# A listed order for the first two token groups, and no unused products at the end

## The chip, the cores and the metric

The kernel runs on one core of a Trainium2 chip. The metric is the device time of one execution in microseconds (us). A core has five engines that work side by side, each through its own instructions in the order in which they were issued: TensorE (PE) for matrix products and transposes, VectorE (DVE), ScalarE (ACT) and GpSimd (POOL) for element-wise work, and SyncE (SP), which here issues the DMA transfers. An engine that comes to an instruction whose input is not ready waits, and everything behind it on that engine waits too. The order of each engine is therefore a design decision of the kernel, and it is what this change is about.

## The reference

The inputs are q, k and v of shape (4, 8, 768, 64), one decay factor per head, and two weight matrices, w_in (512 x 2048) and w_out (2048 x 512). First comes a linear attention with decay, in blocks of 64 tokens:

```python
for b in range(nb):                                   # 12 blocks of 64 tokens
    intra = einsum('bhic,bhjc->bhij', qb, kb) * Dmask # decayed scores inside the block
    intra = einsum('bhij,bhjd->bhid', intra, vb)
    inter = einsum('bhid,bhde->bhie', qb * lam_pow, kv_state)
    out[:, :, sl] = intra + inter
    kv_state = lam_block * kv_state + einsum('bhsd,bhse->bhde', kb * rev_pow, vb)
```

The result is reordered into x, 3072 tokens x 512, and goes through a two-layer network:

```python
h = x @ w_in                  # 3072 x 2048
g = np.maximum(0.01 * h, h)   # leaky relu
return g @ w_out              # 3072 x 512
```

The weights come as float64. The kernel reads them as 64-bit words and builds float32 values from the two halves. Products run in a fast float32 form (fp32r) on operands that are split into a main part (h), a rest (l) and a difference (m), so that one product of the reference becomes three on TensorE.

## The kernel before

**Tiling.** The tokens are cut into 24 chunks of 128 and six groups of four chunks (512 tokens). The 2048 columns of the hidden layer are cut into eight panels of 256.

**Attention.** For a chunk, SP loads k, q (L338, two DMAs each) and v (L388, one DMA). PE transposes k and q (L403; k into a bank b11 or po, q into pt). ACT copies the transposed tiles out (L414 for k, L415 for q), k is multiplied by its decay in place (L419), and q by its powers (L423). PE then makes the scores and the state products into one bank pair, psc (L313, in function scores). DVE multiplies the scores with the decay matrix (L452, into the tile sc), copies or adds the state (L457, L459), and POOL decays the state for the next block (L462). PE makes the outputs into the bank pair po (L313, in function outputs): the block's own part from sc, then in two portions the part from the state, with a tiny copy of po (L491) between the portions. ACT writes the main part of x (xh, L507), DVE the rest and the difference (xl L508, xm L510). From chunk 10 on, k and q are loaded as small sub-blocks instead (L374, many DMAs of 32 or 48 KB) and transposed by DVE (L383).

**Weights of w_in.** For a panel there are two loads of 512 KB (L566). ACT writes three words or half words of each (L578, L580, L582), DVE shifts and adds (L584, L585). The main part of the panel is written by ACT or DVE (wh, L591 or L593), rest and difference by DVE (wl L596, wm L602).

**The first layer, "up".** An up step for a group and a panel (L640) makes two banks out of b10, b11 and b2. Per bank there are products of the h parts and of the l parts, then a scaling by ACT (L658), then products of the m parts, then the leaky relu by ACT (L661) into one of two buffers gs. SP stores the buffer to DRAM (L664, tile g, 512 KB). The two gs buffers alternate, so a leaky relu must wait until the store two steps back has left its buffer.

**The second layer, "down".** From about 340 us on, g is loaded (L675), split (ACT L682, DVE L683 and L685) and multiplied (L700). The results go through ACT L722 and DVE L729 and are stored (L732), at the very end in two stores of half a tile. Before that, w_out is converted like w_in, written to DRAM (L617) and read back (L621) when it replaces the panels of w_in.

**What sets the order.** No engine instruction is issued when its line of Python runs. `add` puts it in a plan with its engine (or a choice of engines), an assumed duration, and the names it reads and writes, and the plan gives it a rank. `emit` then places operations one after the other: each time the one that could start first by the assumed durations, at equal times the one of lower rank. The PE operations of one attention round form a chain, which is kept together: once its first operation is placed, PE takes nothing else until the last. After that, every operation is issued in the order of its assumed start.

**Unused work on PE.** Where the plan sees PE without work before the first product into b10, it puts in unused transposes of 128 x 128 (L266, into b10). There are 30 of them, beside those ahead of the plan. After the last result, 24 unused products of 512 columns (L802) and 8 small ones (L809; 16 rows in the profile) run.

```python
if self.idle is not None and t > soon[e] + 0.4:
    self.idle(int((t - soon[e] - 0.2) / 0.22))
```

## Time and profile before

| what | value |
|---|---|
| median of three runs | 611.83 us (611.01 to 612.28) |
| span of the profiled execution | 610.3 us |
| its own time | not measured apart; the median exceeds its span by 1.5 us |
| mean granted clock of TensorE | 0.997 |
| PE busy | 601.9 us (99%) |
| DVE, ACT, POOL busy | 313.2 us (51%), 269.9 us (44%), 86.6 us (14%) |
| PE idle | 8.4 us, of which 6.6 before 35 us |
| first product of the up steps | starts at 30.41 us |
| scores times decay (L452) of chunks 0 to 3 | start at 8.80, 14.10, 19.04, 26.05 us |
| last result product of PE | ends at 606.28 us |
| last unused product | ends at 609.39 us |

The span runs from the first to the last instruction that the profiler recorded; an execution's time holds a little more. A busy share is the share of the span in which an engine executes something; a matrix product counts as busy until its modelled end. "Granted clock" is the share of full speed at which TensorE was allowed to run. A row such as `L313 <- DMA att<-in_v_dram` names the waiting line and what it waited for. In an instruction's name the tile written stands left of the arrow; att is one large tile that holds all of the attention's data, so a row with att must be told by its line.

### The profile page before, as it was taken

What the parts mean: (1) busy time and instruction counts of PE and PEld (TensorE: products, weight loads), DVE (VectorE), ACT (ScalarE), POOL (GpSimd) and SP (SyncE); (2) the same over time, 40 slices, a digit from 0 to 9 for tenths busy, and PEclk for the clock granted to TensorE, in tenths of its full rate; (3) what the DMA queues carried; (4) which work ended last, traced back from release to release, by engine and by line L of the source; (5) the groups of instructions that cost most, each with busy time, mean ns of one, the idle gap of its engine ahead of it and who ended that gap; (6) DMA issues with size and microseconds to landing.
All of it is one profiled execution on the core that took longest, in us unless ns stands there. A gap on an engine that the chain in (4) does not pass through costs nothing.

```text
span 610.3 us, 13012 instructions
## 1 busy us (share of the span) xinstructions
PE 601.9 (99%) x5426; PEld 497.6 (82%) x5426; DVE 313.2 (51%) x418; ACT 269.9 (44%) x430; POOL 86.6 (14%) x90
## 2 busy tenths in 40 slices
PE   7799999999999999999999999999999999999999
PEld 5688888888888878888788888888888888888887
DVE  5899764334243426326366755545454544636531
ACT  4678974444455646555577522222222313214111
POOL 2564412114133004104000000000000000000000
PEclk9899999999999999999999999999999999999999
DMA  9999775666889878886686843524333343333201
GB/s 201 236 261 263 215 204 126 175 154 176 192 212 245 212 222 219 212 242 212 233 302 219 278 155 103 173 69 139 137 104 134 111 136 111 132 104 126 82 1 69
DMA packets 147754, 105.18 MB, mean 172 GB/s; under 512 B 123632, under 2 KB 124400, under 8 KB 147696
## 3 DMA queue, kind: packets, MB, share of 16 engines
q1 hardware_dynamic: 147552, 104.36, 58.8%
q8 instruction: 42, 0.69, 0.5%
q14 instruction: 16, 0.13, 0.1%
q10 hardware_dynamic: 144, 0.00, 0.0%
HBM read 68.69 MB, written 35.65 MB: 171 GB/s over the span
## 4 chain that ended last, share of the span: by engine, by line
PE 95%; DMA 2%; ACT 1%; DVE 1%; issue 0%; SPq 0%; ACTq 0%
PE b L640 42%; PE b L700 18%; PE po L700 11%; PE psc L700 11%; PE po L313 4%; PE psc L313 4%; PE pt L700 4%; DMA g<-gs 1%; DMA att<-in_v_dram 1%; PE pt L403 1%; DMA att<-in_q_dram 1%; PE po L403 0%; PE psc L802 0%; ACT att L415 0%; PE b L266 0%
## 5 line engine op out<-in xcount | busy, mean ns | idle before, releaser
L682 ACT ACTIVATE xh<-att 128x1024 fp32r<-128x1024 f32 x48 | 50.8, 1060 | 149.1 <-PE b L700 133.6
L683 DVE SCALAR_TENSOR_TENSOR xl<-att,xh 128x1024 fp32r<-128x1024 f32 x48 | 58.7, 1223 | 97.5 <-ACT xh L682 97.5
L640 PE MATMUL b<-xm,wm 128*128 128x512 f32 (+2 forms) x392 | 104.5, 392 | 0.7 <-ACT b L658 0.7
L640 PE MATMUL b<-xh,wh 128*128 128x512 f32 (+2 forms) x392 | 103.2, 386 | 0.8 <-ACT xh L507 0.8
L640 PE MATMUL b<-xl,wl 128*128 128x512 f32 (+2 forms) x392 | 103.4, 387 | 0.0
L640 PEld LDWEIGHTS b<-xh,wh 128*128 128x128 f32 x392 | 72.9, 188 | 16.0 <-ACT xh L507 0.9
L640 PEld LDWEIGHTS b<-xl,wl 128*128 128x128 f32 x392 | 72.7, 188 | 15.1 <-DVE wl L596 0.3
L640 PEld LDWEIGHTS b<-xm,wm 128*128 128x128 f32 x392 | 71.4, 188 | 16.0 <-ACT b L658 1.1
L658 ACT ACTIVATE b<-b 128x512 f32<-128x512 f32 (+2 forms) x97 | 56.1, 580 | 60.6 <-PE b L640 60.5
L661 ACT ACTIVATE gs<-b 128x512 f32<-128x512 f32 (+2 forms) x97 | 57.0, 592 | 44.2 <-PE b L640 38.3
L700 PE MATMUL b<-wh,xh 128*128 128x512 f32 x192 | 74.7, 389 | 0.0
L700 PE MATMUL b<-wl,xl 128*128 128x512 f32 x192 | 74.7, 389 | 0.0
L685 DVE SCALAR_TENSOR_TENSOR xm<-xl,xh 128x1024 fp32r<-128x1024 f32 x48 | 58.7, 1225 | 4.7
L462 POOL TENSOR_TENSOR att<-att 128x256 f32<-128x256 f32 x40 | 34.4, 861 | 58.7 <-DVE att L459 58.7
L700 PEld LDWEIGHTS b<-wh,xh 128*128 128x128 f32 x192 | 36.1, 188 | 7.5
L700 PEld LDWEIGHTS b<-wl,xl 128*128 128x128 f32 x192 | 36.0, 188 | 7.5
L423 POOL TENSOR_TENSOR att<-att 128x512 f32<-128x512 f32 (+1 forms) x20 | 25.3, 1265 | 95.6 <-PE po L313 34.7
L452 DVE TENSOR_TENSOR att<-psc,att 128x512 f32<-128x512 f32 x24 | 16.5, 689 | 43.1 <-PE psc L313 43.1
L584 DVE TENSOR_SCALAR w<-w 128x512 int32<-128x512 int32 x32 | 19.6, 612 | 36.0 <-ACT w L578 35.9
L700 PE MATMUL psc<-wh,xh 128*128 128x512 f32 x96 | 37.3, 389 | 0.0
L700 PE MATMUL psc<-wl,xl 128*128 128x512 f32 x96 | 37.3, 389 | 0.0
L700 PE MATMUL psc<-wm,xm 128*128 128x512 f32 x96 | 37.3, 389 | 0.0
(79 smaller groups left out, 810.4 us busy)
## 6 DMA issues: line engine op xcount, KB each, us to landing
att<-g SPq DMA_DIRECT2D x48, 512.0 KB, 3.3
g<-gs SPq DMA_DIRECT2D x47, 512.0 KB, 4.0
raw<-in_moe_w_in_dram SPq DMA_DIRECT2D x16, 512.0 KB, 5.5
raw<-in_moe_w_out_dram SPq DMA_DIRECT2D x16, 512.0 KB, 4.8
att<-in_k_dram SPq DMA_DIRECT2D x48, 128.0 KB, 4.3
att<-in_v_dram SPq DMA_DIRECT2D x24, 256.0 KB, 4.5
out_dram<-gs SPq DMA_DIRECT2D x23, 256.0 KB, 2.1
wo<-w SPq DMA_DIRECT2D x8, 512.0 KB, 5.9
```

Of the source, the lines that this page charges most:

```text
L313: nc.tensor.matmul(dst[HALF[cols]], lhsT=lhsT[HALF[rows]], rhs=rhs[HALF[rows]], start=start, stop=True, skip_group_check=True)
L423: add(eng, us, lambda: e.tensor_tensor(o, x, _bc(pow_q, 2, 2)[:, :, m, :], op=ALU.mult), ["fq", dep], [f"qsT{i}"])
L452: add("DVE", 0.69, lambda: nc.vector.tensor_tensor(sc, psc[:, :, lower, :], decay, op=ALU.mult), ["psc", "fk"], ["sc"])
L462: add("POOL", 0.7, lambda new=new, j=j: nc.gpsimd.tensor_tensor(state[(j + 1) % 4], new, _bc(lam_c, 2, D), op=ALU.mult), [f"st{j % 4}", "f ...
L584: add("DVE", 0.42, lambda: nc.vector.tensor_scalar(d, d, 3, None, op0=ALU.logical_shift_left), [], [key])
L640: nc.tensor.matmul(dst, lhsT=w[z][:, kk * 2 * P + f * P:kk * 2 * P + (f + 1) * P], rhs=x[z][:, kk, toks], start=start and kk == 0, stop=kk ...
L658: add("ACT", ns, lambda b=b: nc.scalar.activation(out=b, in_=b, func=AF.Copy, bias=0.0, scale=S + 1.0), [], [kb], rank=-1.5)
L661: add("ACT", ns, lambda b=b, r=r: nc.scalar.activation(out=r, in_=b, func=AF.Prelu, bias=0.0, scale=1.0 / WS, alpha=0.01), [kb], [f"gs{jg} ...
L682: add("ACT", 1.05, lambda: nc.scalar.activation(out=h, in_=graw[j], func=AF.Copy, bias=0.0, scale=NEAR), reads, wr("h"))
L683: add("DVE", 1.25, lambda: nc.vector.scalar_tensor_tensor(l, graw[j], 1.0, h.bitcast(F32), op0=ALU.mult, op1=ALU.subtract), reads + [f"rh{ ...
L685: add("DVE", 1.25, lambda: nc.vector.scalar_tensor_tensor(m, l.bitcast(F32), -S, h.bitcast(F32), op0=ALU.mult, op1=ALU.add), [f"rh{j}", f" ...
L700: nc.tensor.matmul(acc[tb][z // 2][:, cols], lhsT=ring[j][z][:, f * T + tb * P:f * T + (tb + 1) * P], rhs=W[pp][z][:, f * d_model:(f + 1) ...
```

## The change

1. A list ORDER names the first 707 operations of the plan (by number, with the engine where there is a choice): all loads, attention rounds, conversions and up steps up to the end of the up steps of groups 0 and 1, with what the list has beside them. `emit` places these first, in this order, each as soon as its inputs and its engine allow by the assumed durations, and then goes on as before with what is left. The issue order of every engine in about the first 200 us is thus the listed one, and what follows is placed from another state of the plan.
2. The attention rounds that the list touches are no longer kept together on PE: transposes and products of other steps can stand between their parts.
3. Unused transposes come only where the list says so (an entry fN puts N of them before the next PE operation): 31 instead of 30.
4. The second set of decay factors is ordered behind the first.
5. The unused products at the end (L802 and L809) are removed.
6. A table OWN is prepared that could give chunks their own buffers; it is empty, and so changes nothing.

Read off the changed program, the loads that SP issues first are q, k, k, q of chunks 0 and 1 and then v of chunk 0, where they were k, q, v, k, q. The numbers and kinds of the other instructions stay. The lines move down by 53 to 58, so L313 becomes L366, L452 L505, L640 L698 and L658 L716.

```diff
+ORDER = """
+3 2 25 0 26 f3 6 4 1 8 f2 5 100 7 9p 10 27 f3 11 49 28 30 f2 12 29 14 48 102 13 15 101 94 16 f1 18 31 104 17 19
+103 32v 50 34 20a 21 33 35 22 23 105 52 37 71 36 51 38 95 72 39 41 56 53 40 42 54 73 43v 98 55 f1 44 96 24 57
...
+637 682 636 699 663 703 503 668 704 571 700 661 640 695 705 641 659 664 678 676 656 706 683 653 671 662 660 672
+673 679
+"""
...
+        self.listed, self.fill = [], {}
...
+        first = {i for i, _ in self.listed}
         for c in self.chains.values():
+            if first.intersection(c):
+                continue
             m = [i for i in c if "PE" in self.ops[i][0]]
...
+        for i, e in self.listed:
+            e = e or next(iter(self.ops[i][0]))
+            assert i in able[e]
+            put(i, e, max(free[e], since(i, e)))
+        while len(done) < n:
...
-                if self.spare in self.ops[i][4]:
+                if self.spare in self.ops[i][4] and not self.listed:
                     self.idle = None
-                if self.idle is not None and t > soon[e] + 0.4:
+                if i in self.fill:
+                    self.idle(self.fill[i])
+                elif not self.listed and self.idle is not None and t > soon[e] + 0.4:
                     self.idle(int((t - soon[e] - 0.2) / 0.22))
...
-    add("DVE", 1.25, factors_q, [], ["fq"])
+    add("DVE", 1.25, factors_q, ["fk"], ["fq"])
...
+    fill = 0
+    for x in ORDER.split():
+        if x[0] == "f":
+            fill = int(x[1:])
+            continue
+        i = int(x.rstrip("avp"))
+        plan.listed.append((i, {"a": "ACT", "v": "DVE", "p": "POOL"}.get(x[-1])))
+        if fill and "PE" in plan.ops[i][0]:
+            plan.fill[i], fill = fill, 0
     plan.emit()
-    a, b = ring[0][0], W[0][0]
-    spare = acc[0] + acc[1]
...
-    strips(2, 6)
-    strips(4, 3)
-    f = graw[0]
-    for _ in range(4):
-        for i in range(2):
-            nc.tensor.matmul(spare[2][HALF[i], 0:C2], lhsT=f[:, 0:C2], rhs=f[:, 0:C2], start=True, stop=True, skip_group_check=True)
```

85 lines of the change are left out of this document (57 added, 28 removed).

## The prediction

> **What bounds the kernel now.** I read the page's busy times first, then the 40 slices, then the waits of TensorE, the table of stretches, and last the timelines of the stretches that were not full.
>
> ```profile
> PE 601.9 (99%) x5426; PEld 497.6 (82%) x5426; DVE 313.2 (51%) x418; ACT 269.9 (44%) x430; POOL 86.6 (14%) x90
> PE   7799999999999999999999999999999999999999
> PEclk9899999999999999999999999999999999999999
> ```
>
> TensorE (PE) is busy for 601.9 of 610.3 us. Only 8.4 us are idle, and the first two slices (to 30.5 us) and the last show it; the lowered clock is early too. The stretches say this in numbers (columns: stretch, length, busy us of PE, PEld, DVE, ACT, POOL, granted clock, DMA share, GB/s):
>
> ```profile
> 15.00:20.00 5.00, 4.33 (x140) 3.25 (x139) 4.61 (x8) 3.78 (x8) 2.64 (x3) 1.00 1.02 227
> 20.00:25.00 5.00, 3.19 (x109) 2.47 (x112) 3.91 (x7) 3.18 (x6) 4.20 (x4) 1.00 1.02 262
> 25.00:30.00 5.00, 4.62 (x115) 3.80 (x104) 3.95 (x6) 2.30 (x5) 1.09 (x3) 0.66 0.89 226
> 35.00:50.00 15.00, 15.00 (x232) 12.33 (x231) 14.07 (x19) 12.37 (x23) 6.86 (x5) 1.00 0.88 250
> 600.00:611.00 11.00, 9.39 (x72) 7.28 (x70) 2.14 (x4) 1.79 (x3) 0.00 (x0) 1.00 0.26 95
> ```
>
> From 35 to 600 us PE idles 0.96 us in all (0.68 in 200-250, 0.28 in 250-300). From 0 to 35 the busy times add up to 28.4, so 6.6 us are idle there. So an order can gain ahead of the first up product (30.41 us) and at the end; elsewhere it can hardly do anything but lose. What holds PE early (columns: waiter, releaser, total us, times, longest), and the way to the first product:
>
> ```profile
> PE psc L313 <- DMA att<-in_v_dram: 1.8, 1, 1.8
> PE psc L313 <- DVE att L459: 1.6, 2, 1.1
> PE b L640 <- ACT xh L507: 0.8, 1, 0.8
> ```
>
> ```profile
> 24.43 1.57 PE L313 MATMUL psc<-att 64*64 64x64 f32 x64 [1.79 <-DMA att<-in_v_dram]
> 25.93 1.33 PE L266 MATMUL b<-att 128*128 128x128 f32 x5
> 27.19 1.46 PE L313 MATMUL po<-att 64*64 64x64 f32 x48
> 28.58 0.66 PE L403 MATMUL pt<-att 128*128 128x128 f32 x4
> 29.16 0.46 PE L313 MATMUL po<-att 64*64 64x64 f32 x16
> 30.41 1.43 PE L640 MATMUL b<-xh,wh 128*128 128x512 f32 x5 [0.78 <-ACT xh L507]
> ```
>
> Chunk 3's state products wait 1.79 us for a v that is the 23rd load on SP's queue; behind them come unused transposes, chunk 3's outputs, a later chunk's transposes and the copy xh. The same shapes are slower here than elsewhere (psc x64 1.57 against 1.09 at 35.26, po x48 1.46 against 0.93 at 20.39, an unused transpose 0.27 in the five here against 0.16 in three at 7.63): the granted clock was halved from 25.0 to 28.4.
>
> **The change, part by part.** The sum is made against the profiled execution: its span is 610.3, and with the 1.5 us by which the median of the runs (611.83) exceeds it, its time is 611.8; the lowest and highest run put that 1.5 at 0.7 and 2.0. The instruction mix stays; the real PE work is equal, so the difference is PE idle, lowered clock and tail. Line numbers are those of before.
>
> *First stage.* The way to the first product is one scores-times-decay (L452) per chunk on DVE, ended at 9.49, 14.79, 19.73 and 26.74 before. In the listed order:
> - v of chunk 0 is the 9th load instead of the 5th. With issues about 0.5 apart from 0.74 and a median of 4.5 to landing it is there at 0.74 + 8 x 0.5 + 4.5 = 9.3. State products (about 0.6), a state copy of 0.41 that now stands ahead, then L452 0.69: ends at 11.1, 1.6 later.
> - Chunk 1: between the two L452 DVE now has L459 0.41, L584 0.84 to 1.28 (as beside POOL), L419 0.67, L423 0.69, L508 0.69, L585 0.69, L459 0.41, L452 0.69, less 8 x 0.085 overlap (0.69 at 14.10, the next at 14.71): 4.4 to 4.9. With some 0.3 of waits, 16.3 (1.5 later).
> - Chunk 2: two L459, L423, the seen copy, L584, L510, L585, L508, L452: 4.2 to 4.6 by the same rows, and the second L459 waits for POOL's decay (L462, 0.86): 22.0 (2.3 later).
> - Chunk 3: L596 1.22 to 1.64, L459, L423, L510, L508, L452, less overlaps: 4.4. It ends at 26.4, 0.3 earlier than before: v of chunk 3 is now the 18th load, so the 1.79 wait goes, and DVE is late next.
> - First product: outputs 0.75 for 24 pieces, seen copy 0.16, the rest 0.31, xh 0.59, and five hand-overs of 0.05 to 0.1: about 28.8 against 30.41. L415 (0.59) and four transposes (0.66) have moved behind the copy. That is 1.6 earlier, but four transposes (0.44 at full clock) are still owed: 1.2 gained with a clean clock.
>
> The clock: in this walk PE idles about 14.7-16.4 and 17.3-19.0, where before had 4.33 busy of 5. Before's halving followed 20-25 with 3.19 of 5 busy and cost 1.0 or a little more (0.48 on psc, 0.53 on po, some on the transposes). That is in the 30.41 already; another such stretch takes the gain to -0.1, and one that hits the serial part more turns it to +1.2. I take -0.3, nearer the row of a half-busy PE; ends -1.2 and +1.2. The 31 unused transposes stand for 30 and are the cover that is cut where the list says so.
>
> [...]
>
> *Conversions near 88 us.* The last m product of group 0 with panel 7 needs wm7 (L602). DVE has L584 (released by ACT at about 83.1), L452, L584, two L585, L593 and L602 ahead: 0.42 + 0.69 + 0.42 + 0.69 + 0.69 + 0.69 + 1.22 = 4.8 if alone, and POOL's decays stand beside them. In before no up product waits for DVE at all. PE waits 0.5; ends 0 and 1.2 (L584 at 1.28, L593 at 1.43). [...]
>
> *Stores between 110 and 137 us.* G stores now stand on SP between the small loads of L374 (about 0.5 per issue). Two buffers gs: L661 of an up step waits for the store two steps back, then L658, then PE. Before has this chain at 213.8:
>
> ```profile
> 214.79 5.73 DMA g<-gs
> 220.52 0.02 issue
> 220.54 0.04 ACTq L661
> ...
> 223.35 0.44 ACT gs L661
> 223.79 0.49 ACT b L658
> 224.28 0.04 issue
> 224.33 2.12 PE b L640 x8
> ```
>
> The 5.73 us store cost PE 0.7 there. In the listed stretch the chain closes at a landing of about 3.0 and costs about 2 at the median of 4.0, 3 at 4.5. Stores without small loads beside them took 2.7 to 3.0 in the trace, those with them 3.98 and 4.18. I take 3.4, near the 3.3 median of the 512 KB loads of G, and so 0.8; ends 0 and 3.
>
> *After the list, about 333 us.* The rest is placed greedily, from another state. ACT then gets, between the scalings of two up banks, L591, L578, L580, L582, L682 and L661: 1.06 + 0.66 + 0.78 + 0.77 + 1.06 + 0.60 - 5 x 0.10 = 4.43. Before has only L591, L658, L682, L661 there (331.56 to 334.56, nothing waits), with L578 to L582 one bank earlier. PE has four groups of products to cover it, 4 x 0.907 = 3.63; with two hand-overs it waits about 1.0 (0.8 to 1.1).
>
> *End.* Before, the two last stores land at 608.55 and 609.01, the unused products end at 609.39 and the exit follows. Without them the stores end the kernel: -0.4 (-0.5 to 0). No product follows them, so a lower clock there hurts nothing. The transposes and copies moved within the listed part beyond these places cost nothing, covered by a PE that is full in every stretch of 35 to 200; a cover too thin shows as PE idle there.
>
> Sum: -0.3 + 0.5 + 0.8 + 1.0 - 0.4 = +1.6, so 611.8 + 1.6 = 613.4.
>
> **Rivals.**
> - *Faster: the first stage gains more.* For it: 6.6 of the 8.4 us idle lie there, the v wait is gone, and my walk adds DVE's worst rows at L584. Against it: three L452 come later. It decides when first up products start before about 28.0 at full clock (30.41 - 0.44 - 28.0 = 2.0 gained) and stores land in 3.0: -2.0 + 1.0 - 0.4 = -1.4, 610.4.
> - *No difference: the parts cancel.* Clean clock (-1.2), wm7 in time, stores at 3.2 (0.4), +1.0, -0.4: -0.2, 611.6. This is also the case of an order that moves work PE never waits for.
> - *Clearly slower: the store chain.* Stores at 4.5 give 3 us instead of 0.8; with the rest as summed 615.6. For it: 3.98 and 4.18 beside small loads. Against it: only one 0.7 us wait of this kind in all of before.
> - *The clock.* A second halved stretch of 3.4 us before 30 us costs about 1.1 more: 614.5.
>
> **How the numbers follow.** Likeliest 613.4 (0.40); store chain 0.09 and second halving 0.05 beside it; parts cancel 0.24; faster 0.22. A change within 0.2% (1.2 us, 610.6 to 613.0) can't be told from none. Slower by more 0.54, within 0.24, faster 0.22. The range: low end at the faster rival's first stage taken 0.5 further (products from 27.5), 609.9; high end at +1.2 + 1.2 + 1.5 + 1.1 - 0.4 = +4.6, 616.4. The likeliest case's own range is 613.0 to 614.8.
>
> **What would show it.** First stage: L452 ends near 11, 16, 22, 26.4, the first up product near 28.8, no wait for in_v at chunk 3, and the clock of the slices to 30 us. Conversions: a wait of an up product for DVE's wm L602 near 88. Stores: up products waiting for ACT's L658 between 110 and 140, behind a G store of 4 us or more. Greedy rest: a wait of about 1 us for L658 near 333. End: the last work a store about 1.5 us before the span's end. I am wrong if PE stays full from 35 us on while the first product starts before 28 (faster), or if the first stage alone loses over 2 us.

## The result and the profile after

The changed kernel takes 613.3 us (median of six runs, 612.87 to 614.21), against 611.12 us for the kernel before in the same session (six runs, 610.33 to 612.28). The ratio is 1.0034 with a 95% interval of 1.0024 to 1.0045: slower by about 2.2 us. The time is 0.1 us beside the predicted 613.4, but the forecast stood on a base of 611.8, and six runs put that base at 611.12: the forecast change was +1.6, the measured one +2.2. The profiled execution is one of the six: 613.25 us, span 611.43. From here on lines are those of the changed kernel unless "before" is said: L266 is now L319, L313 L366, L403 L456, L414 L467, L415 L468, L419 L472, L423 L476, L452 L505, L462 L515, L491 L544, L578 L631, L640 L698, L658 L716, L661 L719. (A correction to what stands ahead: the 30 and 31 unused transposes include the 11 that run ahead of the plan.)

The busy times and slices of the page, after:

```profile
PE 600.1 (98%) x5387; PEld 496.0 (81%) x5387; DVE 304.8 (50%) x418; ACT 268.0 (44%) x430; POOL 83.7 (14%) x90
...
PE   7899999999999999999999999999999999999997
...
PEclk9899999999999999999999999999999999999999
```

PE has 1.8 us less work than before, since the unused products are gone; their last slice now shows 7. The second slice is fuller than before (8 for 7), and the lowered clock is still there. The table of stretches, after (columns as before: stretch, length, busy us of PE, PEld, DVE, ACT, POOL, granted clock, DMA share, GB/s):

```profile
15.00:20.00 5.00, 2.60 (x85) 1.88 (x88) 3.41 (x9) 2.95 (x6) 2.25 (x3) 0.99 0.85 171
20.00:25.00 5.00, 4.83 (x133) 4.17 (x127) 4.82 (x9) 2.78 (x5) 2.78 (x3) 0.67 1.06 298
25.00:30.00 5.00, 4.62 (x154) 3.52 (x145) 3.69 (x7) 2.75 (x6) 1.60 (x2) 1.00 1.01 256
35.00:50.00 15.00, 15.00 (x235) 12.34 (x234) 10.57 (x14) 12.52 (x23) 10.71 (x8) 1.00 0.74 190
300.00:350.00 50.00, 49.22 (x217) 40.41 (x217) 30.24 (x31) 32.88 (x53) 0.00 (x0) 1.00 0.75 264
600.00:611.00 11.00, 7.81 (x39) 6.43 (x37) 2.83 (x5) 2.04 (x4) 0.00 (x0) 0.97 0.26 95
```

The half-busy stretch has moved from 20-25 to 15-20, and the halved clock follows it one stretch earlier (0.67 in 20-25, where before had 0.66 in 25-30). From 35 us on PE again hardly idles: the largest hole is 0.78 in 300-350. The waits of PE, after (waiter, releaser, total us, times, longest):

```profile
PE po L366 <- DVE att L544: 1.6, 1, 1.6
...
PE po L366 <- DVE att L505: 1.4, 3, 0.7
PE b L698 <- ACT gs L719: 0.8, 1, 0.8
PE psc L366 <- DMA att<-in_v_dram: 0.6, 1, 0.6
PE psc L366 <- ACT att L468: 0.5, 1, 0.5
```

The 1.79 us wait for chunk 3's v is gone; a wait of 1.58 for DVE, in chunk 1's outputs, stands in its place. The timeline of PE around it and at the first up product, after:

```profile
17.55 0.33 PE L319 MATMUL b<-att 128*128 128x128 f32 x1
19.46 0.46 PE L366 MATMUL po<-att 64*64 64x64 f32 x16 [1.58 <-DVE att L544]
19.74 1.84 PE L366 MATMUL psc<-att 64*64 64x64 f32 x64
...
29.07 0.66 PE L456 MATMUL pt<-att 128*128 128x128 f32 x4
29.85 2.11 PE L698 MATMUL b<-xh,wh 128*128 128x512 f32 x8
```

What DVE waited for is on ACT. ACT's timeline, after:

```profile
16.98 0.68 ACT L631 ACTIVATE w<-raw 128x512 f32<-128x512 f32 x1 [2.60 <-DMA raw<-in_moe_w_in_dram]
17.57 0.56 ACT L467 COPY att<-b 128x512 f32<-128x512 f32 x1
18.03 0.58 ACT L468 COPY att<-pt 128x512 f32<-128x512 f32 x1
```

The list puts a conversion of w_in ahead of the copies of a chunk's k and q. Its load is late, ACT stands 2.60 us, and the copies behind it wait though their own data are ready. DVE's timeline, after:

```profile
18.65 0.69 DVE L476 TENSOR_TENSOR att<-pt,att 128x512 f32<-128x512 f32 x1 [1.46 <-ACT att L468]
19.26 0.15 DVE L544 COPY att<-po 128x2 f32<-128x2 f32 x1
```

On DVE L476 (chunk 2's q) is released by L468 at 18.65, the tiny copy L544 (of chunk 1's outputs) stands behind L476 and ends at 19.41, and PE waits for that.

**Where the 1.14 us of the two profiles lie.** The first product starts 0.56 earlier (29.85 against 30.41), the last result product starts 1.52 later (607.53 against 606.01), and what comes after it is 0.38 shorter (3.90 against 4.28). So the stretch from the first to the last product took 577.68 instead of 575.60 us, 2.08 more. Counted from the start times of PE's instructions:

| between first and last product | us |
|---|---|
| four transposes that before had done ahead of the first product | +0.44 |
| more changes between transposes, 64 x 64 products and 512-column products | +0.10 |
| weight loads that come late (17 groups instead of 7; 1.49 us instead of 0.59) | +0.90 |
| wait at 336.4 us, behind the list | +0.95 |
| gap at 63.8 us | +0.37 |
| wait at 224.3 us, which before has and after has not | -0.84 |
| the rest | +0.16 |

The third row needs its lines. Two groups of products in the timeline of PE, after:

```profile
117.66 1.07 PE L698 MATMUL b<-xl,wl 128*128 128x512 f32 x4
118.56 1.19 PE L698 MATMUL b<-xh,wh 128*128 128x512 f32 x4
```

And weight loads in the timeline of PEld, after:

```profile
118.56 0.76 PEld L698 LDWEIGHTS b<-xh,wh 128*128 128x128 f32 x4 [0.25 <-ACT gs L719]
...
121.42 0.76 PEld L698 LDWEIGHTS b<-xh,wh 128*128 128x128 f32 x4 [0.27 <-ACT gs L719]
```

A group whose weights load behind the products of the group before takes 1.07. Where the bank that it writes is freed late by the leaky relu (L719), the loads wait too and the group takes 1.19: its second product comes 0.10 to 0.11 late. Nine of the 17 late groups wait for the leaky relu; of the seven before none does. (Three of the 17, and four of the seven, are the first up product's group and groups behind narrower products.) The page of waits doesn't list this, since PE itself starts on time; it shows as an extra tenth in the duration of a group. So the listed order has more places in which the next products into a bank stand only one group (0.907 us) behind its m products.

### The profile page after: what moved, and what is told of

It is laid out like the page before. It is cut to its first block, busy times and chain, and to the rows that moved or that the text cites. A ratio compares the mean times of both kernels' runs of the same rounds, so it can differ in the third digit from the quotient of the medians.

```text
span 611.4 us, 12907 instructions
## 1 busy us (share of the span) xinstructions
PE 600.1 (98%) x5387; PEld 496.0 (81%) x5387; DVE 304.8 (50%) x418; ACT 268.0 (44%) x430; POOL 83.7 (14%) x90
## 4 chain that ended last, share of the span: by engine, by line
PE 95%; DMA 2%; ACT 1%; SPq 1%; issue 1%; DVE 0%; DVEq 0%; ACTq 0%
PE b L698 44%; PE b L758 18%; PE psc L758 11%; PE po L758 11%; PE po L366 4%; PE psc L366 4%; PE pt L758 4%; DMA raw<-in_moe_w_in_dram 1%; SPq L391 1%; DMA att<-in_v_dram 1%; PE pt L456 1%; PE po L456 0%; ACT att L467 0%; PE b L456 0%; ACT low L633 0%
## 5 line engine op out<-in xcount | busy, mean ns | idle before, releaser
L698 PE MATMUL b<-xh,wh 128*128 128x512 f32 (+2 forms) x392 | 105.1, 392 | 1.1 <-ACT gs L719 0.8
L698 PE MATMUL b<-xl,wl 128*128 128x512 f32 (+2 forms) x392 | 103.3, 388 | 0.0
L698 PE MATMUL b<-xm,wm 128*128 128x512 f32 (+2 forms) x392 | 102.5, 390 | 0.0
L698 PEld LDWEIGHTS b<-xh,wh 128*128 128x128 f32 x392 | 71.6, 188 | 17.9 <-ACT gs L719 3.3
L698 PEld LDWEIGHTS b<-xl,wl 128*128 128x128 f32 x392 | 72.7, 188 | 15.3 <-DVE att L512 0.3
L698 PEld LDWEIGHTS b<-xm,wm 128*128 128x128 f32 x392 | 71.7, 188 | 15.2 <-ACT b L716 0.8
L716 ACT ACTIVATE b<-b 128x512 f32<-128x512 f32 (+2 forms) x97 | 56.2, 582 | 56.0 <-PE b L698 55.7
L719 ACT ACTIVATE gs<-b 128x512 f32<-128x512 f32 (+2 forms) x97 | 56.8, 590 | 43.8 <-PE b L698 37.9
L476 POOL TENSOR_TENSOR att<-att 128x512 f32<-128x512 f32 (+1 forms) x20 | 27.0, 1353 | 92.0 <-DVE att L436 32.2
L505 DVE TENSOR_TENSOR att<-psc,att 128x512 f32<-128x512 f32 x24 | 16.4, 684 | 43.2 <-PE psc L366 43.0
L758 PE MATMUL b<-wm,xm 128*128 128x512 f32 x96 | 37.4, 389 | 0.0
L758 PE MATMUL po<-wl,xl 128*128 128x512 f32 x96 | 37.3, 389 | 0.0
```

What stands on the lines that cost most here:

```text
L476: add(eng, us, lambda: e.tensor_tensor(o, x, _bc(pow_q, 2, 2)[:, :, m, :], op=ALU.mult), ["fq", dep], [f"qsT{i}"])
L505: add("DVE", 0.69, lambda: nc.vector.tensor_tensor(sc, psc[:, :, lower, :], decay, op=ALU.mult), ["psc", "fk"], ["sc"])
L698: nc.tensor.matmul(dst, lhsT=w[z][:, kk * 2 * P + f * P:kk * 2 * P + (f + 1) * P], rhs=x[z][:, kk, toks], start=start and kk == 0, stop=kk ...
L716: add("ACT", ns, lambda b=b: nc.scalar.activation(out=b, in_=b, func=AF.Copy, bias=0.0, scale=S + 1.0), [], [kb], rank=-1.5)
L719: add("ACT", ns, lambda b=b, r=r: nc.scalar.activation(out=r, in_=b, func=AF.Prelu, bias=0.0, scale=1.0 / WS, alpha=0.01), [kb], [f"gs{jg} ...
L758: nc.tensor.matmul(acc[tb][z // 2][:, cols], lhsT=ring[j][z][:, f * T + tb * P:f * T + (tb + 1) * P], rhs=W[pp][z][:, f * d_model:(f + 1) ...
```

## The experiments

Each kernel ran beside the kernel before, on one chip in one session. There were several sessions, so compare the ratios, not the medians. The columns: median of the runs, ratio to the kernel before with its 95% interval, and of the one profiled execution the span, the starts of the first up product and of the last result product and the time between them.

| kernel | median us | ratio | span | first | last | between |
|---|---|---|---|---|---|---|
| before | 611.12 to 611.87, by session | 1 | 610.29 | 30.41 | 606.01 | 575.60 |
| after | 613.30 | 1.0034 (1.0024 to 1.0045) | 611.43 | 29.85 | 607.53 | 577.68 |
| no_spare | 611.04 | 0.9992 (0.9978 to 1.0006) | 610.43 | 30.56 | 606.53 | 575.97 |
| unused_in_before | 611.54 | 0.9995 (0.9980 to 1.0011) | 609.74 | 29.32 | 605.84 | 576.52 |
| xl_ahead | 612.46 | 1.0013 (0.9999 to 1.0027) | 610.49 | 29.73 | 606.58 | 576.85 |
| copy_ahead | 613.13 | 1.0025 (1.0014 to 1.0037) | 612.29 | 30.09 | 608.39 | 578.29 |
| more_unused | 613.68 | 1.0042 (1.0024 to 1.0060) | 611.30 | 29.55 | 607.40 | 577.84 |
| relu_ahead_333 | 613.38 | 1.0022 (1.0009 to 1.0034) | 609.93 | 29.28 | 606.02 | 576.74 |
| list_to_first | 613.08 | 1.0020 (1.0005 to 1.0034) | 611.25 | 30.06 | 607.35 | 577.29 |
| decay_ahead | 615.49 | 1.0054 (1.0033 to 1.0076) | 613.07 | 28.92 | 609.16 | 580.24 |
| list_and_decay | 612.41 | 1.0015 (0.9999 to 1.0031) | 611.03 | 30.01 | 607.11 | 577.11 |
| later_bank_use | 613.16 | 1.0019 (1.0008 to 1.0030) | 612.51 | 30.56 | 608.59 | 578.03 |
| after_again | 613.49 | 1.0040 (1.0026 to 1.0054) | 610.76 | 29.69 | 606.86 | 577.16 |
| before_again | 612.86 (one run) | | 611.05 | 29.05 | 606.77 | 577.72 |

**no_spare: the end alone.** The kernel before without its unused products at the end.

```diff
-    a, b = ring[0][0], W[0][0]
-    spare = acc[0] + acc[1]
...
-    strips(2, 6)
-    strips(4, 3)
-    f = graw[0]
-    for _ in range(4):
-        for i in range(2):
-            nc.tensor.matmul(spare[2][HALF[i], 0:C2], lhsT=f[:, 0:C2], rhs=f[:, 0:C2], start=True, stop=True, skip_group_check=True)
```

> The kernel before without the unused products after the last result; nothing else changes. Own theory: the two last stores end the kernel instead of the unused products (609.01 against 609.39 in the profile of before), so about 0.4 us less, ratio to before about 0.9993, and the last store lands about 1.3 us ahead of the end of the span. Rival: the exit has its own length whatever PE does, and the time stays within 0.1 us. Second rival: without the products the clock of the last real ones falls and the time grows.

The tail behind the last result product is 3.90 us, as after, against 4.28: -0.38 in the profile. The runs say 0.9992, which is -0.5 us with nothing excluded between -1.3 and +0.4. The order is the one of before, and the profile has the 224 us wait (0.60) and one of 0.78 for wl at 48.65. So the missing products are no cost. What makes the changed kernel slower is the order.

**copy_ahead: ACT's conversion behind the copies.** The one step that the wait at 19.46 us points to: the conversion L631 (entry 95) moves behind L467 and L468.

```diff
-38 95 72 39 41 56 53 40 42 54 73 43v
+38 72 39 41 56 53 40 42 54 95 73 43v
```

> The changed kernel with one entry of the list moved: on ACT the first part of a panel's conversion (L631, which waited 2.60 us for its load at 16.98) stands behind the two copies of chunk 2's transposes (L467, L468) instead of ahead of them. Theory that the wait of ACT carries through DVE (L476, L544) to PE's 1.58 us wait at 19.46: the copies run at 15 to 16.5, the wait shrinks to 0.3 or less, the scores times decay of chunk 2 end at about 21.3 instead of 22.7, the first up product starts near 28.9 instead of 29.85, and the time falls by 0.7 to 1.2 us against the changed kernel's 613.3. Rival, that DVE's own work or the halved clock sets chunk 2 and 3: the wait at 19.46 shrinks but the first product stays at 29.6 to 29.9, and the time stays within 0.3 us.

The wait is gone: the same 16 products start at 18.52 with no wait. PE's timeline in copy_ahead shows what came instead:

```profile
17.30 0.93 PE L366 MATMUL po<-att 64*64 64x64 f32 x48 [1.44 <-DVE att L505]
...
18.52 0.46 PE L366 MATMUL po<-att 64*64 64x64 f32 x16
...
26.45 0.46 PE L366 MATMUL psc<-att 64*64 64x64 f32 x14 [0.83 <-issue]
```

With no 2.60 us hole on ACT, chunk 1's scores-times-decay becomes the late one (1.44, against 0.69 in the changed kernel). PE waits 0.97 at 13.19 (against 0.47) for a copy that stands behind the first w_in conversion, whose load came 0.6 later in this execution (11.38 against 10.76). A gap of 0.83 at 26.45 waits for nothing that the profile shows, and a wait of 0.90 for ACT's xh at 249.6, which the changed kernel's profile does not have, lengthens the stretch behind the first product. The first product comes at 30.09, 0.24 later than after, and the time is no better: 1.0025 against 1.0034, inside each other's intervals. The cause of the wait at 19.46 is shown; that it costs time at the end is not. What was taken off ACT was lost in other waits.

**more_unused: the holes filled.** The list of after with more unused transposes ahead of the operations where PE stood.

```diff
-103 32v 50 34 20a
+103 32v 50 f3 34 20a
...
-38 95 72 39 41 56 53
+38 95 72 39 f5 41 56 53
...
-98 55 f1 44 96
+98 55 f9 44 96
...
-83 f4 87 169
+83 f6 87 169
```

> The changed kernel with more unused transposes ahead of four PE operations: 3 instead of 0 before the scores of chunk 1, 5 instead of 0 before chunk 1's outputs, 9 instead of 1 before their second part (the 1.58 us wait at 19.46), 6 instead of 4 before chunk 3's outputs. Theory that PE's idle time between 14.7 and 19.5 halves the clock from 20.0 to 23.4: no slice of the first 30 us shows a granted clock under 0.95, the state products of chunk 2 take 1.1 instead of 1.84, the first product starts at 29.0 to 29.3 instead of 29.85, and the time is 0.5 to 0.9 us below 613.3. Rival, that the halving has another cause: it stays, and the time is the same or up to 0.3 us longer by the unused work. Third: the halving goes, but DVE and ACT set the stage, and the first product moves by less than 0.3 us.

No stretch at half clock is left ahead of the first product. PE's timeline, more_unused:

```profile
19.58 1.11 PE L366 MATMUL psc<-att 64*64 64x64 f32 x64
...
29.55 1.65 PE L698 MATMUL b<-xh,wh 128*128 128x512 f32 x6
```

The 64 products that took 1.84 after take 1.11, a gain of 0.73. The first product starts 0.30 earlier than after, the last one 0.13 earlier, and the runs say 1.0042 (1.0024 to 1.0060). Restoring the clock ahead of the first product bought nothing that can be measured; the nine of its twelve runs whose granted clock is 0.999 or more have a median of 613.22. DVE is still behind, so the faster products only wait for it longer (three waits for L505, 2.2 us in sum, against 1.4).

**relu_ahead_333: ACT's order behind the list.** A leaky relu near 333 us moves ahead of the conversions between which the planner had put it.

```diff
         self.timeline = sorted(done)
+        on_act = [m for m, x in enumerate(self.timeline) if x[3] == "ACT"]
+        relu = [m for m in on_act if any(y.startswith("gs") for y in self.ops[self.timeline[m][2]][4])][91]
+        first = max(m for m in on_act if m < relu and any(y.startswith("w32") for y in self.ops[self.timeline[m][2]][4]))
+        late, line = set(), []
+        for m in range(first, relu):
+            i = self.timeline[m][2]
+            if m in on_act or self.ops[i][2] & late:
+                late.add(i)
+            else:
+                line.append(self.timeline[m])
...
+        line += [self.timeline[relu]] + [x for x in self.timeline[first:relu] if x[2] in late]
+        self.timeline[first:relu + 1] = line
```

> The changed kernel with ACT's order changed at one place: the leaky relu that frees a bank at about 336 us stands ahead of the conversion of w_out and the split of g that were ahead of it (with the DVE work that reads them behind). Theory: PE's wait of 0.95 us at 336.4 goes, and with the work that follows hidden, the time falls by 0.8 to 1.0 us against 613.3. Rival, that the wait only moves to the next bank or to the first products of the second layer, which need the conversion: the time stays within 0.3 us.

First the chain that it cuts, in ACT's timeline, after:

```profile
331.99 1.06 ACT L645 ACTIVATE wh<-att 128x1024 fp32r<-128x1024 f32 x1 [0.25 <-PE b L698]
332.96 0.64 ACT L631 ACTIVATE w<-raw 128x512 f32<-128x512 f32 x1
333.51 0.79 ACT L633 ACTIVATE low<-raw 128x512 uint16<-128x512 uint32 x1
334.16 0.77 ACT L635 ACTIVATE low<-raw 128x512 f16<-128x512 f32 x1
334.80 1.03 ACT L740 ACTIVATE xh<-att 128x1024 fp32r<-128x1024 f32 x1
335.74 0.57 ACT L719 ACTIVATE gs<-b 128x512 f32<-128x512 f32 x1
```

Six instructions from 331.99 to 336.31, 4.32 us, and PE's products into the freed bank start at 336.36. With the relu first, at 331.89, PE still waits, for a scaling that now stands behind the conversions (the code added shifts the lines by 13: L729 is L716). PE's timeline, relu_ahead_333:

```profile
335.78 2.11 PE L711 MATMUL b<-xm,wm 128*128 128x512 f32 x8 [0.36 <-ACT b L729]
```

The wait fell from 0.95 to 0.52, counted from the starts of the products. The time between first and last product is the shortest of all listed orders (576.74), but the runs, 1.0022 (1.0009 to 1.0034), can't tell half a microsecond from the 1.0034 of after. The term is confirmed by the profile, not by the runs.

**list_to_first: the list only as far as the first stage.** The list ends ahead of entry 159, after 117 operations (not 94, as the expectation says); everything behind it is placed greedily.

```diff
-111 88 70 89a f1 90 113 91 172 92 159 173 108 154
...
-673 679
+111 88 70 89a f1 90 113 91 172 92
```

> The changed kernel with the list cut after the first 94 operations that stand ahead of the first up product; everything after is placed greedily, as before. Own theory: the listed part after the first product costs PE about 1.1 us without a wait that the table of waits shows (seven blocks of transposes between products instead of one, and fourteen weight loads that come late instead of six), on top of the 0.95 us at 336. Here PE has two such blocks, so from the first product to the last PE takes 575.9 to 576.6 us, against 577.68 in the changed kernel and 575.60 before, and the time is 611.4 to 612.0, 1.3 to 1.9 below the changed kernel. Rival: the extra PE time belongs to the transposes that are still owed and to the state that any list leaves behind, so PE takes 577.2 or more, and the time is 612.8 or more.

1.0020 (1.0005 to 1.0034): slower than before, and not told apart from after. Ten late loads, fewer than the 17, but waits come back that the longer list does not have: 0.28 at 34.20, 0.84 at 38.84, 0.39 at 56.73 and 0.23 at 225.65. Three of PE's waits in list_to_first:

```profile
13.89 0.93 PE L366 MATMUL psc<-att 64*64 64x64 f32 x32 [1.64 <-ACT att L468]
...
38.84 1.20 PE L698 MATMUL b<-xm,wm 128*128 128x512 f32 x4 [0.67 <-ACT b L716]
...
56.73 2.11 PE L698 MATMUL b<-xh,wh 128*128 128x512 f32 x8 [0.23 <-ACT wh L645]
```

So the listed first stage followed by the greedy rest loses about as much as the whole list, but in other places.

**unused_in_before: the clock in the order of before.** no_spare with seven more unused transposes ahead of the state products that waited for v.

```diff
+                if i == 80:
+                    self.idle(7)
```

> The kernel before without the unused products at the end, and with seven more unused transposes ahead of chunk 3's state products, where PE waits 1.79 us for v. Theory that a stretch in which PE is less than about half busy halves the clock: the halved stretch from 25.0 to 28.4 us does not come, psc x64 takes 1.1 instead of 1.57, and the first product starts at 29.2 to 29.8 instead of 30.41; the time is 0.6 to 1.1 us below the kernel before with the tail's 0.4 in it. Rival: the halved stretch stays or only moves, the first product starts at 30.3 to 30.6, and only the tail's 0.4 is gained. Second rival: the halving goes, but the copy xh that follows it waits for something else, and the first product moves by less than 0.3 us.

The clock stays full in the profile, and the first product starts at 29.32 instead of 30.41. That the unused transposes kept it full is not shown: the order of before loses the clock in only 16 of 101 runs, and before_again, with nothing added, starts at 29.05. Nor is a limit at about half busy: PE was busy 3.19 of 5 us ahead of the halving in before, and 3.13 ahead of none in before_again. Of these 1.1 us nearly all is gone by the last product (605.84 against 606.01). PE's timeline, unused_in_before:

```profile
31.95 0.66 PE L405 MATMUL po<-att 128*128 128x128 f32 x4 [0.52 <-DVE xl L510]
...
48.10 1.20 PE L642 MATMUL b<-xl,wl 128*128 128x512 f32 x4 [0.61 <-DVE wl L598]
```

PE reaches the next transposes before DVE has read the bank (xl), and the second panel's products before DVE has written wl. Both waits aren't in the profile of before, where PE is 1.1 us later. The ratio is 0.9995 (0.9980 to 1.0011). The start of the first product alone is thus not what sets the end: here an earlier start met DVE's conversions, which had not moved.

**decay_ahead: more help for the first stage.** copy_ahead, POOL's decay of k for chunk 3 (entry 78) ahead of the state decay (61), and unused transposes where PE stands.

```diff
-103 32v 50 34 20a
+103 32v 50 f4 34 20a
...
-38 95 72 39 41 56 53 40 42 54 73 43v
+38 72 39 f6 41 56 53 40 42 54 95 73 43v
...
-59 61 75 109 107 78 77 64
+59 75 109 107 78 61 77 f4 64
```

> The changed kernel with the copies ahead of the conversion on ACT (as in copy_ahead), the decay of chunk 3's k (L472 on POOL, which took 2.01 to 2.04 us beside DVE's work, ahead of the state products of chunk 3) ahead of chunk 2's first state decay on POOL, and 13 more unused transposes in the waits of 10 to 23 us. Theory that POOL's late decay sets chunk 3 now: the state products of chunk 3 start at 23.9 to 24.3 instead of 24.6 to 26.4 (copy_ahead), no halved stretch, and the first product starts at 28.7 to 29.2. The time is 612.2 to 612.8, since all that follows the first product is that of the changed kernel (577.7 to 578.0 from first to last product). Rival: POOL's decay is as slow there and delays the state decay instead; the first product stays at 29.5 to 30.1, and the time at 613.0 or more.

The first product starts at 28.92, the earliest of all, at full clock, and the kernel is the slowest of all: 1.0054 (1.0033 to 1.0076). PE's timeline, decay_ahead:

```profile
62.88 0.44 PE L366 MATMUL po<-att 64*64 64x64 f32 x6 [1.96 <-issue]
```

PE stood 1.96 us with no releaser in the profile. A 16 KB packet on the queue that brings instructions started at 60.52 and took 0.96 us, with the DMA engines at a share of 1.02 from 59.0 to 60.9. That a late fetch of PE's instructions is the cause is likely from these times and from the other gaps of this kind (last section), not shown. Two waits of 0.95, at 276.5 and 338, come on top. All six runs took 614.74 us or more; whether the stall came in each is not on record.

**list_and_decay: both.** decay_ahead's list, cut ahead of entry 159 as in list_to_first.

> The two together: the first stage of decay_ahead, and the list cut at the first up product, so that the rest is placed greedily. If both theories hold, the first product starts at 28.7 to 29.2, PE takes 575.9 to 576.6 from the first product to the last, and the time is 610.5 to 611.2, 0.3 to 1.0 us below the kernel before (ratio 0.9984 to 0.9995). If the first theory fails, 612.2 or more; if the second fails, 611.3 to 612.0.

1.0015 (0.9999 to 1.0031), first product 30.01, 577.11 to the last. It is the least slow of the listed orders, and told apart from decay_ahead alone. The stall of 1.96 did not come. The first product starts 1.1 later than in decay_ahead though the order up to it is the same; 0.75 of that is a gap with no releaser at 26.14.

**later_bank_use: the late loads.** relu_ahead_333, and two groups of products moved on PE, so that the next use of a bank stands one group later.

```diff
+        for op, other, later in ((559, 590, 0), (685, 632, 1)):
+            queue["PE"].remove(op)
+            queue["PE"].insert(queue["PE"].index(other) + later, op)
```

> The changed kernel with the repair of relu_ahead_333, and with two product groups moved on PE in the listed part, so that the next products into a bank come two groups after its m products instead of one at three places (118.9, 121.8 and 141.1 us in the changed kernel); no other engine's order changes. Theory that a cover of one group (0.907 us) is too thin for the leaky relu (0.60), the hand-overs and the weight load, and that each such place costs 0.10 to 0.11 us without a wait of PE: the late weight loads fall from 15 (relu_ahead_333) to 12, the second product of these three groups starts 0.23 us after the first instead of 0.33, and from the first product to the last PE takes 0.3 less than in relu_ahead_333 if the waits are otherwise alike. In the time of many runs 0.3 us can hardly be told: 612.2 to 613.2. Rival: the extra tenth belongs to the leaky relu's place on ACT or to the group itself, and the three stay.

The late loads go from 15 in relu_ahead_333 to 12 (1.32 to 1.02 us). The three that went are those at 118.6, 121.4 and 130.2 us in the changed kernel, and only two of them are places that the expectation named: the third named, at 140.8, still takes 1.19 (142.14 here), and the one at 130.2 went because its group was moved. At the first place shown above, whose group now stands one group later, the timeline of PE in later_bank_use (L723 is L698):

```profile
120.31 1.07 PE L723 MATMUL b<-xm,wm 128*128 128x512 f32 x4
121.22 1.07 PE L723 MATMUL b<-xh,wh 128*128 128x512 f32 x4
```

And that of PEld:

```profile
121.00 0.87 PEld L723 LDWEIGHTS b<-xh,wh 128*128 128x128 f32 x4
```

The load starts 0.22 ahead of its group, and the group takes 1.07 again instead of 1.19; the second place's group (123.03) does the same. The mechanism is shown at these places: what stands between the m products of a bank and its next use decides it. The 0.3 us is too small for the runs (1.0019, 1.0008 to 1.0030), and this execution lost 1.4 us in new waits elsewhere (1.05 at 72.35 and 0.32 at 248.5, both with no releaser).

**after_again and before_again: how much of a profile comes back.** Both kernels unchanged, profiled a second time.

> The changed kernel as it is, for a second profile and more times on the chip of the other runs. What belongs to the order itself should return: the first product between 29.2 and 30.1, a wait of 0.9 to 1.0 us near 336, 16 to 18 late weight loads, the tail of 3.9. What belongs to the one execution should not: the 0.37 us at 63.8. The ratio to the kernel before should again lie between 1.002 and 1.0045.

> The kernel before as it is, for a second profile. If the wait near 224 us (0.84 in the first profile, 0.60 and 0.45 in two kernels with the same order there) belongs to the order, it returns with 0.4 to 0.9 us; the first product starts between 30.2 and 30.8, the clock is halved from about 25 us, 6 or 7 weight loads come late. If it belongs to single executions, PE waits less than 0.3 us there.

After: 1.0040 (1.0026 to 1.0054) in another session. The wait behind the list came back (0.94 at 335.7), so did the late loads (16) and the halved clock at 19.8; the gap at 63.8 did not. Before: the second profile differs much more. PE's timeline, before_again:

```profile
24.40 1.16 PE L313 MATMUL psc<-att 64*64 64x64 f32 x64 [1.71 <-DMA att<-in_v_dram]
...
29.05 2.11 PE L640 MATMUL b<-xh,wh 128*128 128x512 f32 x8 [0.78 <-ACT xh L507]
...
31.68 0.66 PE L403 MATMUL po<-att 128*128 128x128 f32 x4 [0.52 <-DVE xl L508]
...
42.17 0.83 PE L403 MATMUL po<-att 128*128 128x128 f32 x4 [0.76 <-DMA att<-in_k_dram]
```

The same wait for v, yet no halved clock after it, and the first product 1.36 us earlier than in the first profile. The last one is 0.76 later. A wait for xl (0.52) follows, as in unused_in_before, then one for a k load that took 7.01 us, and a gap of 0.56 at 65.5 with no releaser. The wait near 224 us came back (0.72). All five profiles of this order have it, with 0.32 to 0.84, so it belongs to the order. The halved stretch and the late first product, which the expectation also gave to the order, do not.

**xl_ahead: the next wait of unused_in_before.** DVE's xl moves ahead of a conversion of weights (wm) that stood before it.

```diff
+        queue["DVE"].remove(92)
+        queue["DVE"].insert(queue["DVE"].index(108), 92)
```

> The kernel unused_in_before with one DVE operation moved: the rest of chunk 3 (xl, L510, 0.68 us) ahead of panel 1's wm (L604, which took 1.98 us there beside POOL), where PE waited 0.52 us for xl at 31.95. Nothing else changes its place. Theory that DVE's whole work from 15 to 50 us, 4.8 to 5.0 of 5 us in unused_in_before, holds PE, and that an earlier first product is given back whatever stands first: the 0.52 goes, the wait for wl at 48.1 (0.61) stays or grows to 0.6 to 0.9, and the time stays within 0.4 us of unused_in_before (ratio 0.9990 to 1.0005). Rival, that only the order of these two held PE: the 0.52 goes, the wait at 48 does not grow, PE takes 575.8 to 576.0 from the first product to the last instead of 576.52, and the time falls by 0.5 to 0.7 (ratio 0.9984 to 0.9988), the only version here that would beat both kernels.

The wait for xl is gone: the four transposes start at 31.69 with none. But PE then stands 1.3 at 64.11, of which 1.1 has no releaser, and 0.45 at 38.92, and the ratio is 1.0013 (0.9999 to 1.0027), not below unused_in_before. The wait for wl at 48.1 went as well, which the theory did not expect, and the time from the first product to the last (576.85) is not the rival's either. So removing the first wait was possible, and worth nothing to the end.

## Why the prediction was right, step by step

The total was right, and that is in part luck. It came out of terms of which some were right, two did not come at all, and two were not in it. The base was off too. The prediction gave the profiled execution of before 611.8 us, its span and 1.5. In the 13 profiles that have both numbers on record, an execution takes 1.78 to 1.82 us more than its span, so that one took about 612.1, 1.0 above the median of six runs. A base 0.7 too high and a change 0.6 too small nearly cancel.

**First stage (-0.3 in the prediction).** The walk of the four scores-times-decay was right in form: ends at 11.13, 16.64, 22.74 and 27.41 against the forecast 11.1, 16.3, 22.0 and 26.4, late by 0.7 and 1.0 from chunk 2 on. The v wait went, as said, and DVE was late next. (Chunk 3's v is the 22nd load, not the 18th, and was the 24th, not the 23rd; it landed at 21.14 instead of 24.30.) A stretch at half clock came again, 19.9 to 23.3. The first product is 0.56 earlier and four transposes are owed (0.44): -0.12, against -0.3. The step that differs is "the second L459 waits for POOL's decay" in chunk 2. It did not wait for POOL. DVE stood 1.46 us for ACT's copy L468, behind the conversion L631 that waited 2.60 us for its load, which the walk, made for DVE and SP, didn't hold. This wait alone does not make the chunk late, though: in copy_ahead it is gone, and the chunk's L505 ends at 22.44, only 0.30 earlier, since DVE's xm (L563) takes 1.54 there instead of 0.68, while POOL runs L472. And the premise "an order can gain ahead of the first up product" is too strong: unused_in_before, decay_ahead and before_again start the products 1.1 to 1.5 us earlier than the first profile of before, and end from 0.2 earlier to 3.2 later than it.

What decides whether the clock is halved is not shown; the same program can have a halved stretch or not. Each one ahead of the first product lasts 3.41 us; before had one at 25.0 behind a wait of 1.79, before_again had none behind a wait of 1.71 with PE busy 3.13 of 5 us. With a clean clock the prediction gave this stage 1.2 instead of 0.3. That did not come: the clock was halved at 19.9, behind holes of 1.58 us at most. More_unused shows that a full clock would not have brought the other 0.9 either: its first product starts at 29.55, 0.30 earlier than after.

**Conversions near 88 us (+0.5).** It was 0. The timeline of DVE, after:

```profile
88.54 1.22 DVE L656 SCALAR_TENSOR_TENSOR wm<-wl,wh 128x1024 fp32r<-128x1024 f32 x1
```

And the timeline of PE, after:

```profile
89.98 1.97 PE L698 MATMUL b<-xm,wm 128*128 128x512 f32 x8
```

wm7 is written at 89.76, and its products start at 89.98 with no wait. The upper end took L584 at 1.28, as in the profile of before at 42.84 beside L419 on POOL, against 0.42 at 50.12 with POOL idle; here the two of this chain (L637) took 0.47 at 85.02 and 0.69 at 86.01, both with POOL at work. The chain was as near as the walk said (0.2 us), but on the side that costs nothing, the lower end that the prediction gave.

**Stores between 110 and 137 us (+0.8, up to 3).** It was 0. PE waits for nothing from 100 to 145 us. The size of 3.4 us for a store is not what failed: the three that start between 110 and 137 us landed after 2.93, 3.83 and 5.31 us, and after 3.25, 4.10 and 5.16 in after_again. What failed is the step "the chain closes at a landing of about 3.0 and costs about 2 at the median of 4.0". Landings of 3.8 and 5.3 cost nothing here. From 115 to 145 us the leaky relus on ACT stand for PE, and only one, at 140.15, for a DMA, 0.37 us.

**After the list, near 333 us (+1.0).** 0.95, and 0.94 in after_again. ACT's chain took 4.32 against the 4.43 summed from the rows. PE met it at its last instruction, the leaky relu, at 336.4 (not at the scaling, which the prediction named as the sign). This is the one term beyond the start of the kernel that was named with its place and came.

**End (-0.4).** -0.38 in the profile, and the same tail of 3.90 in no_spare. The last work is a store, as said.

**What the sum lacked.** Late weight loads, +0.90: the prediction counted waits of PE and took products that start on time as free. And the wait at 224 us of before, which was read as an example of the store chain and then kept: after does not have it, -0.84. "A cover too thin shows as PE idle there" is the sentence that failed: a thin cover shows first as groups of 1.19 instead of 1.07.

So 1.3 us of predicted waits did not come, nor 0.84 that before had. Late loads (0.90), the gap at 63.8 (0.37), changes and the rest (0.26) and a smaller gain in the first stage (0.18) came in their place, and the two profiles differ by 1.14 instead of 1.6. The medians differ by 2.2. The missing 1.0 us is the distance of before's profiled execution (about 612.1) from the median of its runs (611.12); after's (613.25) lies at its median (613.30).

The clock seems to have a part in the 2.2 us. Before's first profile has a halved stretch, and this is its rarer case: of 101 single runs of before in the sessions of the experiments, 16 show a granted clock of 0.997 and 85 show 1.000 (a stretch of 3.41 us at half clock takes 0.0028 off the mean). In each of the four sessions the runs at 0.997 took longer on average, by 0.4, 1.3, 0.6 and 0.5 us (0.65 weighted). Of the changed kernel 13 of 15 runs show 0.997 or less, three of them 0.994, the mark of two such stretches. Sixteen stretches in 15 runs against 16 in 101, at 0.65 us each, make 0.6 of the 2.2 us, an estimate. The larger part seems not to be clock: the two runs of the changed kernel at 0.999 and 1.000 took 613.35 and 613.29.

**The rivals.** "Faster" fell with the first stage: its condition, products before 28.0 us, was not met by any kernel here, and decay_ahead, the nearest (28.92), is the slowest. "No difference" is excluded by the interval. "The store chain" did not form. "A second halved stretch" did not come in the profiles, but one run of six, and two of nine in after_again, show a granted clock of 0.994; they took 613.75, 615.42 and 615.98.

**What is shown of the whole.** All nine ratios with the listed start lie at 1.0015 to 1.0054; the three with the order of before at 0.9992 to 1.0013, though single intervals of the two overlap. No single place carries the 2 us, and taking one away let another stand in its place.

## What to carry to other kernels

Where one engine is busy 98% of the span, count its instructions' start times, not only its waits: a weight load that came a little late cost 0.10 to 0.11 us per group here and showed in no list of PE's waits, and 17 of them cost 1.49 us, more than any wait of the changed kernel behind the first product. Ask of a new order not only what it removes but what is one step behind: an earlier first product was nearly all given back in every variant here, often to engines whose work had not moved. And profile both kernels twice before explaining differences of 1 us, since of the three gaps behind the first stage one did not come back. Read the granted clock of every run as well: it showed that the one profile of before was not its usual case.

## What the runs showed of the hardware

- **The clock at equal idleness.** In the profiles the halved stretch ahead of the first product came in seven of eight that left PE's holes as they were, and in none of the six with unused work or earlier copies in them. Its length was always 3.41 us, its start anywhere from 14.2 to 25.0. The single runs say how often it comes. A granted clock of 0.997 or less stands in 16 of 101 runs of before. It stands in 36 of 51 runs of the four kernels that have the listed first stage as it is (the changed kernel, 13 of 15; relu_ahead_333, later_bank_use and list_to_first), and in 9 of 42 of the four that fill its holes or take the long one away (more_unused, copy_ahead, decay_ahead, list_and_decay). So with the listed order these edits made the halving rarer.
- **DVE and POOL side by side.** L472 on POOL takes 1.05 us at 17.91 after, with DVE idle until 18.65, and 2.04 at 22.80, with DVE at work throughout; wm on DVE takes 1.22 at 88.54 after, with POOL idle, and 1.98 at 29.32 in unused_in_before, with L425 and L464 on POOL beside it. Not every instruction takes longer: at 102.80 after, wm on DVE takes 1.22 beside L472 on POOL, which takes 2.08. Why one of the two takes longer, and which, no run here shows.
- **Changing the shape of PE's work.** Behind a block of transposes the second 512-column product comes 0.09 us late, each time, and behind a block of 64 x 64 products 0.11 us, 21 times in each kernel. The listed order, which lets transposes stand between products, has 7 such changes where before has 1.
- **Gaps with no releaser.** 1.96 us at 60.92 in decay_ahead, 1.05 at 71.30 in later_bank_use, 1.1 at 63.0 in xl_ahead, 0.83 at 25.6 in copy_ahead: they come in stretches with full DMA engines (shares of 0.98 to 1.15 in the 1.6 to 2.3 us ahead of these four), at other places in each execution, and no edit of the order here was aimed at them. In all fourteen profiles there are eleven such gaps of 0.15 us or more behind 9 us, the 63.8 of after among them. Each time a packet of 16 KB on the queue that brings instructions had ended 1.2 to 1.7 us before PE went on. A profile of after has 42 such packets and one such gap, so a packet alone does not make one; no run here changed the fetching.
